# Loading a weight matrix with a cast in flight by GpSimd's software DMA instead of staging it and casting on engines

## The chip, the cores and the metric

The kernel runs on one core of a Trainium2 chip. The metric is device time in microseconds (us), the median of several executions. One execution of each kernel is also recorded by the hardware profiler; its span, from the first instruction to the last, is about 2 us shorter than the timed execution. In the profile PE is TensorE's matmuls, PEld its weight loads, DVE is VectorE, ACT ScalarE, POOL GpSimd, SP SyncE, and a "q" behind a name (SPq, POOLq) marks a queue of DMA issues. L1268 is line 1268 of the kernel. Lines of the changed kernel stand 4 further down than the same lines before, up to the place of the main edit (L911 before is L915 after); from there on the numbers agree again.

## The reference

Eight batches of linear attention (no softmax, RMS norm per head) followed by a residual MLP mixer with affine scalings. Cut to what matters:

```python
def _attn_ref(q, k, v, g_norm):                     # (8, 8, 576, 64)
    kv = np.einsum('bhsd,bhse->bhde', k, v)
    out = np.einsum('bhsd,bhde->bhse', q, kv)
    rms = np.sqrt(np.mean(out * out, axis=-1, keepdims=True) + 1e-06)
    return out / rms * g_norm

def _moe_ref(x, alpha1, beta1, w_tok, alpha2, beta2, w_ch1, w_ch2, lam):
    a1 = alpha1 * x + beta1                         # x: (8, 576, 512)
    tok = np.einsum('ts,bsd->btd', w_tok, a1)       # token mixing
    u = x + lam * tok
    a2 = alpha2 * u + beta2
    ch = np.maximum(a2 @ w_ch1, 0.0) @ w_ch2        # w_ch1 (512, 2048), w_ch2 (2048, 512)
    return u + lam * ch
```

All inputs are fp32. The two channel products run in bf16 on TensorE, so W_ch1 must be cast, and W_ch2 is multiplied by lam and cast at once.

## The kernel before

The program is not written in issue order. Operations are recorded with costs, priorities and dependencies, and a scheduler in the kernel's own Python simulates the engines with these costs and fixes a **static order** for each engine. Every engine then works through its list strictly in order and waits on semaphores where a dependency is on another engine or a DMA. An operation that may run on several engines is given to whichever seems best.

The scheduler's model of DMA is a single line of work that serves loads one after the other in the order of issue:

```python
if pick.lat is not None:                 # a DMA
    if e == "SP":
        dma_free = max(dma_free, t + (2.5 if t < 3 else 1.25)) + pick.lat
        pick.end = dma_free + 1.3        # when it believes the data is there
    ...
```

Both weights of the channel MLP pass through one staging tile of three 1 MB blocks. Four column slices of W_ch1 come first, then four row blocks of W_ch2:

```python
stg = sb("stg", [128, 3, 4, 512], F32)
w1  = sb("w1",  [128, 4, FF], BF16)
w2  = sb("w2",  [128, 16, DM], BF16)
...
order = ["k0", "v0", "q0", "k1", "t0", "v1", "q1", "t1",       # SyncE's first loads
         "w0", "g", "w1", "w2", "Bk", "Bv", "t2", "w3", "Bq", "lam", "a2", "w4",
         "w5", "w6", "w7"]
...
def load_w(i):
    if i < 4:                                                   # W_ch1
        P.op("SP", 0.6, lambda e: e.dma_start(stg[:, i % 3], moe_w_ch1[...]),
             w=[("stg", i % 3)], dma_us=2.6, at=sp["w%d" % i])
        for dj in range(4):                                     # 16 casts in all
            P.op({"ACT": ..., "POOL": 0.66, "DVE": ...}, 0, lambda e, dj=dj: copy(
                e, w1[:, dj, 512 * i:512 * i + 512], stg[:, i % 3, dj]), ...)
    else:                                                       # W_ch2
        n = i - 4
        P.op("SP", 0.6, lambda e: e.dma_start(stg[:, i % 3], moe_w_ch2[...]),
             w=[("stg", i % 3)], dma_us=2.6, at=sp["w%d" % i])
        for hh in range(4):                                     # 16 multiplies, VectorE or GpSimd
            P.op(dve_pool(512), 0, lambda e, hh=hh: e.tensor_tensor(
                out=w2[:, 4 * n + hh, :], in0=stg[:, i % 3, hh], in1=lam_bc[:], op=ALU.mult),
                r=[("stg", i % 3), "lam"], w=[("w2p", n, hh)], pri=60, after=u0, port=True)
```

VectorE's list holds the operations that TensorE waits for: it evacuates `ps`, the tiles that TensorE's matmuls write, for the first channel product (`ht`, L911), for K^T V (`kvr`, L494), for Q^T (`qtr`, L494) and for the small token weights (`wt`, L494). Where nothing useful is ready early on, the scheduler puts filler matmuls (L1334, 45 in the trace, 0.27 us each) on TensorE so that it does not idle.

Of the kernel before, what the change touches and what calls it, by code (L numbers as in the profile page):

```python
# [54 lines left out]
class Prog:  # L55
# [79 lines left out]
    def schedule(self):  # L135
# [83 lines left out]
        while left:  # L219
            progressed = False  # L220
            for e, q in queues.items():
                while q and free[e] <= t + 1e-9:
# [64 lines left out]
                    if pick.lat is not None:  # L287
                        if e == "SP":
                            dma_free = max(dma_free, t + (2.5 if t < 3 else 1.25)) + pick.lat
                            pick.end = dma_free + 1.3  # L290
                        else:
                            pick.end = t + pick.lat + 3.0
                    else:
                        pick.end = free[e] + (0.35 if e == "PE" else 0.15)
# [22 lines left out]
    def synchronize(self):  # L317

        known = {}
        pos = {}  # L320
        pool = None
        for o in self.sequence:
            e = self.queue_of(o.eng)
            if e == "POOL":

                if pool is not None:
                    o.deps.add(pool)
                pool = o
            o.pos = pos.get(e, 0)
            pos[e] = o.pos + 1  # L330
            k = known.setdefault(e, {})
            need = {}
            for y in o.deps:
                ye = self.queue_of(y.eng)
                if y.lat is not None:
                    key, v = ("dma", y.idx), 1
                else:
                    key, v = ye, y.pos + 1
                    if ye == e and e == "PE":
                        continue  # L340
                if v > need.get(key, (0, None))[0]:
                    need[key] = (v, y)
            for key, (v, y) in sorted(need.items(), key=lambda kv: -kv[1][1].end):
                if k.get(key, 0) >= v:
                    continue
                o.waits.append(y)
                y.inc = True
                for kk, vv in y.clock.items():
                    if vv > k.get(kk, 0):
                        k[kk] = vv  # L350
            o.clock = dict(k)
            if o.lat is not None:
                o.clock[("dma", o.idx)] = 1
                o.inc = True
            else:
                o.clock[e] = o.pos + 1

    def emit(self):
        nc = self.nc
        sems = {e: self.stack.enter_context(nc.semaphore("s_" + e)) for e in self.COMPUTE}  # L360
        count = {e: 0 for e in self.COMPUTE}
        val = {}
        dma = []
        for o in self.sequence:
            if o.lat is not None:

                for s in dma:
                    if o.clock.get(("dma", s[2]), 0):
                        break
                else:  # L370
                    s = [self.stack.enter_context(nc.semaphore("d%d" % len(dma))), 0, 0]
                    dma.append(s)
                s[1], s[2] = s[1] + 16, o.idx
                val[o.idx] = (s[0], s[1])
            elif o.inc:
                count[o.eng] += 1
                val[o.idx] = (sems[o.eng], count[o.eng])
        block = self.stack.enter_context(nc.Block("main"))

        @block.gpsimd  # L380
        def _(gps):
            for o in self.sequence:
                eng = self.eng[o.eng]
                for y in o.waits:
                    eng.wait_ge(*val[y.idx])
                ins = o.fn(eng)
                if o.lat is not None:
                    ins.then_inc(val[o.idx][0], 16)
                elif o.inc:
                    ins.then_inc(sems[o.eng], 1)  # L390
            for s in dma:
                nc.sync.wait_ge(s[0], s[1])
# [11 lines left out]
def bass_transnormer_attn__then__resmlp_affine_kernel(  # L404
# [15 lines left out]
    with ExitStack() as stack:  # L420
# [55 lines left out]
        def dve_us(n, mode=1):  # L476
            return 0.16 + n / 960.0 / mode

        def act_us(n):
            return 0.19 + n / 1200.0  # L480
# [554 lines left out]
        def params():  # L1035
# [34 lines left out]
            for x, (p, c) in enumerate(((64, 4), (0, 9))):  # L1070
                for i in range(2):
                    P.op("SP", 0.6, lambda e, i=i, p=p, c=c: e.dma_start(
                        rt[p + i:p + i + 1, c, :].rearrange("o (j p) -> o j p", p=128),
                        ebf[:, i, :]), r=["ebh", "ebl", "rtz"], w=[("rtc", x, i)], dma_us=0.05,
                        at=sp["w0"] + 0.1 + 0.01 * (2 * x + i))
                P.lastw[("rtc", x)] = [y for i in range(2) for y in P.lastw[("rtc", x, i)]]

        def params_late():
            for key in ("e1r", "lamr", "gr", "er", "ebh", "ebl", ("pc", 0), ("pc", 1)):
                for n in range(4):  # L1080
# [2 lines left out]
                            P.readers.get(key, []) + P.lastw[key])  # L1083

        order = ["k0", "v0", "q0", "k1", "t0", "v1", "q1", "t1",
                 "w0", "g", "w1", "w2", "Bk", "Bv", "t2", "w3", "Bq", "lam", "a2", "w4",
                 "w5", "w6", "w7"]
        sp = {n: i - 1000.0 for i, n in enumerate(order)}

        load_params()  # L1090
# [150 lines left out]
        for key in [("wst", tc) for tc in range(4)]:  # L1241
            for o in P.readers.get(key, ()):
                for j in range(16):
                    P.readers.setdefault(("ht", j), []).append(o)
                    for i in range(2):
                        P.readers.setdefault(("hth", j, i), []).append(o)

        def load_w(i):
            if i < 4:
                P.op("SP", 0.6, lambda e: e.dma_start(  # L1250
                    stg[:, i % 3], moe_w_ch1[:, 512 * i:512 * i + 512].rearrange(
                        "(j p) f -> p j f", p=128)), w=[("stg", i % 3)], dma_us=2.6,
                    at=sp["w%d" % i])
                for dj in range(4):
                    P.op({"ACT": act_us(512), "POOL": 0.66, "DVE": dve_us(512, 1.6)}, 0,
                         lambda e, dj=dj: copy(
                        e, w1[:, dj, 512 * i:512 * i + 512], stg[:, i % 3, dj]),
                        r=[("stg", i % 3)], w=[("w1p", i, dj)], at=-960.0 + i, port=True)
                P.lastw[("w1", i)] = [y for dj in range(4) for y in P.lastw[("w1p", i, dj)]]
                bias_groups(i)  # L1260
            else:
                n = i - 4
                P.op("SP", 0.6, lambda e: e.dma_start(
                    stg[:, i % 3], moe_w_ch2[512 * n:512 * n + 512, :].rearrange(
                        "(j p) c -> p j c", p=128)), w=[("stg", i % 3)], dma_us=2.6,
                    at=sp["w%d" % i])
                for hh in range(4):
                    P.op(dve_pool(512), 0, lambda e, hh=hh: e.tensor_tensor(  # L1268
                        out=w2[:, 4 * n + hh, :], in0=stg[:, i % 3, hh], in1=lam_bc[:],
                        op=ALU.mult), r=[("stg", i % 3), "lam"], w=[("w2p", n, hh)], pri=60,  # L1270
                        after=u0, port=True)
                P.lastw[("w2", n)] = [y for hh in range(4) for y in P.lastw[("w2p", n, hh)]]
# [98 lines left out]
```

## Time and profile before

| before | value |
|---|---|
| time, median of 3 first runs (range) | 363.12 us (363.04 to 363.73) |
| span of the profiled run, mean granted TensorE clock | 362.2 us, 0.995 |
| TensorE idle between 15.5 and 58.3 us (start-up with W_ch1) | 0.56 us |
| first weight load of the second channel layer | 58.10 us |
| end of the last matmul of that layer | 358.56 us |
| between these two | 300.47 us |

The layer's first 512-column matmul starts 0.21 us after its weight load. The lines of the page and of the stretches are shown and read in the prediction below. One view that the prediction did not use belongs here, because the outcome turns on it: the order of VectorE around the W_ch2 multiplies. Columns are start, length from the first start to the last end, engine, line, operation, output and inputs, count, and in brackets the idle time just before with what ended it.

```profile
37.58 4.20 DVE L911 TENSOR_SCALAR ht<-ps,bias 128x256 bf16<-128x256 f32 x6 [0.48 <-PE ps L952]
...
43.23 0.69 DVE L1268 TENSOR_TENSOR w<-stg,xtl 128x512 bf16<-128x512 f32 x1 [0.26 <-DMA stg<-in_moe_w_ch_dram]
...
43.91 1.89 DVE L1268 TENSOR_TENSOR w<-stg,xtl 128x512 bf16<-128x512 f32 x3
45.83 0.88 DVE L494 CAST kvr<-ps 64x256 fp32r<-64x256 f32 x2
```

The first multiply comes behind six evacuations of the first channel layer in a row, and three more just ahead of those, and its block lands 0.26 us after VectorE is free for it. The match is close, and VectorE loses almost nothing. In the staging view that the prediction quotes in part, the whole wait of VectorE for W_ch2 blocks is 0.3 us.

### The profile page before, as it was taken

The numbers are of one execution on the slowest core, as the hardware profiler recorded it, in microseconds if no ns is written. First come the engines' busy times: TensorE is split into PE (matmuls) and PEld (weight loads), VectorE is DVE, ScalarE is ACT, GpSimd is POOL, SyncE is SP. The second block draws the span as 40 slices with busy tenths as digits, with TensorE's granted clock in tenths as the row PEclk, the third lists the DMA queues.
The fourth block names the chain that finished last, engine by engine and source line by source line (L and its number), as shares of the span: only waits on it lengthen the run. The fifth ranks groups of instructions, "written<-read, shape, count | busy, mean of one in ns | idle before, by whom it ended". The sixth has DMA issues, their size and how long they took to land.

```text
span 362.2 us, 7967 instructions
## 1 busy us (share of the span) xinstructions
PE 353.6 (98%) x3543; PEld 213.6 (59%) x3335; DVE 207.1 (57%) x321; ACT 147.5 (41%) x262; POOL 113.1 (31%) x93
## 2 busy tenths in 40 slices
PE   7999999999999999999999999999999999999995
PEld 5888774467754554457744554457744554457644
DVE  3555799962876288723974289714883288620021
ACT  2576267037750168007830167007720156007500
POOL 4377078410252006700381016800751006300000
PEclk9899999999999999999999999999999999999999
DMA  7999996067947694667926692686746510341023
GB/s 282 364 375 338 376 365 223 0 73 128 315 156 119 107 313 162 88 128 117 381 47 134 111 352 88 116 119 194 288 66 128 115 29 2 72 93 24 2 58 87
DMA packets 67558, 59.17 MB, mean 163 GB/s; under 512 B 45552, under 2 KB 45828, under 8 KB 67524
## 3 DMA queue, kind: packets, MB, share of 16 engines
q1 hardware_dynamic: 67472, 58.66, 59.7%
q8 instruction: 27, 0.44, 0.5%
q14 instruction: 7, 0.06, 0.0%
q10 hardware_dynamic: 52, 0.01, 0.0%
HBM read 38.60 MB, written 9.44 MB: 133 GB/s over the span
## 4 chain that ended last, share of the span: by engine, by line
PE 93%; DMA 3%; DVE 1%; SPq 1%; issue 1%
PE ps L986 34%; PE ps L936 19%; PE ps L921 14%; PE ps L785 8%; PE ps L602 5%; DMA vf<-in_v_dram 3%; PE ps L397 2%; PE ps L682 2%; PE ps L1144 2%; PE ps L798 1%; PE ps L819 1%; PE ps L570 1%; PE ps L952 1%; DVE w L1268 1%; SPq L506 1%
## 5 line engine op out<-in xcount | busy, mean ns | idle before, releaser
L986 PE MATMUL ps<-w,ht 128*128 128x512 bf16 (+1 forms) x569 | 125.8, 373 | 1.8 <-issue 1.0
L986 PEld LDWEIGHTS ps<-w,ht 128*128 128x128 bf16 x592 | 56.8, 98 | 64.0 <-issue 1.2
L910 ACT ACTIVATE ht<-ps,bias 128x640 bf16<-128x640 f32 (+2 forms) x100 | 74.1, 744 | 45.8 <-PE ps L936 37.9
L936 PE MATMUL ps<-a2t,w 128*128 128x320 bf16 x512 | 71.5, 299 | 0.0
L760 POOL TENSOR_TENSOR xm<-xm,g_bc 128x1024 f32<-128x1024 f32 (+1 forms) x17 | 35.0, 2061 | 111.4 <-DVE rt L757 109.3
L936 PEld LDWEIGHTS ps<-a2t,w 128*128 128x128 bf16 x512 | 49.4, 98 | 20.2
L997 DVE TENSOR_TENSOR xm<-ps,xm 128x512 f32<-128x512 f32 (+1 forms) x33 | 22.2, 673 | 56.5 <-PE ps L986 56.4
L921 PE MATMUL ps<-a2t,w 128*128 128x512 bf16 x231 | 53.3, 380 | 0.9 <-DVE small L737 0.5
L633 ACT ACTIVATE kvd<-ps 64x256 bf16<-64x256 f32 x24 | 9.1, 378 | 101.2 <-PE ps L602 101.0
L731 DVE TENSOR_REDUCE small<-sq 128x16 f32<-128x1024 f32 (+3 forms) x30 | 25.1, 849 | 24.9 <-ACT sq L729 24.7
L921 PEld LDWEIGHTS ps<-a2t,w 128*128 128x128 bf16 x240 | 22.6, 98 | 25.7 <-DVE xm L753 0.7
L785 PE MATMUL ps<-rt,wt 128*128 128x512 bf16 x140 | 31.4, 379 | 0.0
L911 DVE TENSOR_SCALAR ht<-ps,bias 128x512 bf16<-128x512 f32 (+2 forms) x32 | 22.9, 725 | 11.4 <-PE ps L921 5.1
L729 ACT ACTIVATE sq<-ps 128x1024 f32<-128x1024 f32 (+3 forms) x30 | 21.6, 735 | 10.2 <-PE ps L397 8.2
L769 DVE TENSOR_TENSOR xm<-ps,xm 128x512 f32<-128x512 f32 x28 | 19.1, 686 | 8.0 <-PE ps L785 7.9
L785 PEld LDWEIGHTS ps<-rt,wt 128*128 128x128 bf16 x140 | 13.7, 98 | 16.5
L771 POOL TENSOR_TENSOR a2b<-xm,a_bc 128x512 bf16<-128x512 f32 x11 | 17.7, 1610 | 17.6 <-DVE xm L769 17.6
L534 POOL TENSOR_TENSOR qs<-qf,qs 128x512 bf16<-128x512 f32 x12 | 15.2, 1266 | 25.5 <-ACT qs L493 24.5
L997 DVE TENSOR_TENSOR xtl<-ps,xtl 128x512 f32<-128x512 f32 x4 | 2.8, 691 | 35.5 <-PE ps L986 35.5
L753 DVE TENSOR_TENSOR xm<-ps,small 128x1024 f32<-128x1024 f32 (+1 forms) x20 | 20.0, 1004 | 0.2
L602 PEld LDWEIGHTS ps<-vf,kf 64*64 64x64 f32 x1152 | 18.0, 137 | 3.5 <-issue 2.5
L602 PE MATMUL ps<-vf,kf 64*64 64x64 f32 x1152 | 19.3, 223 | 0.3 <-DMA vf<-in_v_dram 0.2
(105 smaller groups left out, 337.1 us busy)
## 6 DMA issues: line engine op xcount, KB each, us to landing
stg<-in_moe_w_ch_dram SPq DMA_DIRECT2D x8, 1024.0 KB, 10.9
kf<-in_k_dram SPq DMA_DIRECT2D x7, 1152.0 KB, 6.2
vf<-in_v_dram SPq DMA_DIRECT2D x7, 1152.0 KB, 9.2
qf<-in_q_dram SPq DMA_DIRECT2D x7, 1152.0 KB, 9.8
out_dram<-xm SPq DMA_DIRECT2D x62, 128.0 KB, 2.4
kf<-in_k_dram SPq DMA_DIRECT2D x2, 576.0 KB, 5.8
vf<-in_v_dram SPq DMA_DIRECT2D x2, 576.0 KB, 7.1
qf<-in_q_dram SPq DMA_DIRECT2D x2, 576.0 KB, 8.5
```

Source lines behind the costliest of these rows:

```text
L602: m = e.matmul(t.ap(slice(64 * i, 64 * i + 64))[:, y, 64 * x_:64 * x_ + 64], kf[rows, x, c], vf[rows, x, c], start=(c == 0), stop=(c == 8) ...
L729: P.op("ACT", act_us(64 * m), lambda e: e.activation(both(sqv), raw(), ACT.Square), r=[t], w=[("sq", sqs)])
L731: P.op("DVE", dve_us(64 * m), lambda e: e.tensor_reduce(out=smv, in_=sqv, axis=AX.X, op=ALU.add), r=[("sq", sqs)], w=[("sm", sms)], pri=-20)
L753: P.op("DVE", dve_us(64 * m), lambda e: e.tensor_tensor(out=x3, in0=raw(), in1=inv(), op=ALU.mult), r=[t, ("sm", sms)], w=xk, pri=-200)
L760: P.op(dve_pool(64 * m) if b < 2 else "POOL", pool_us(64 * m), lambda e: e.tensor_tensor(out=x3, in0=x3, in1=gb, op=ALU.mult), r=xk + ["g" ...
L785: m = e.matmul(t.flat(), wt[:, sc if sc < 4 else 4 + b % 2, 128 * c:128 * c + 128], rt[:, rs(b, sc), :], start=(sc == 0), stop=(sc == 4))
L910: return e.activation(dst, src(), ACT.Relu, bias=bi)
L911: return e.tensor_scalar(out=dst, in0=src(), scalar1=bi, scalar2=0.0, op0=ALU.add, op1=ALU.max)
L921: m = e.matmul(t.flat(), w1[:, dj, 128 * fj:128 * fj + 128], a2t[:, dj, 0:512], start=(dj == 0), stop=(dj == 3))
L936: m = e.matmul(t.ap()[:, i, 0:320], w1[:, dj, 128 * fj:128 * fj + 128], a2t[:, dj, 320 * i:320 * i + 320], start=(dj == 0), stop=(dj == 3))
L986: m = e.matmul(t.flat()[:, 0:m_], ht[:, fj, 128 * c:128 * c + 128], w2[:, fj, lo:hi], start=(fj == 0), stop=(fj == 15))
L997: P.op("DVE", dve_us(m_), lambda e: e.tensor_tensor(out=x, in0=t.flat()[:, 0:m_], in1=x, op=ALU.add), r=[t] + keys, w=keys)
```

## The change

The intent is to give up the staging and the 16 engine casts for W_ch1. GpSimd issues four DMAs that read fp32 and write bf16 straight into the weight tile. The staging tile is then free for W_ch2 from the start, and the scheduler may move everything else into the room. Its core:

```diff
                         if e == "SP":
                             dma_free = max(dma_free, t + (2.5 if t < 3 else 1.25)) + pick.lat
                             pick.end = dma_free + 1.3
+                        elif e == "POOL":
+                            dma_free = max(dma_free, free[e] + 1.0) + pick.lat
+                            pick.end = dma_free + 1.3
...
         order = ["k0", "v0", "q0", "k1", "t0", "v1", "q1", "t1",
-                 "w0", "g", "w1", "w2", "Bk", "Bv", "t2", "w3", "Bq", "lam", "a2", "w4",
-                 "w5", "w6", "w7"]
+                 "g", "t2", "Bk", "Bv", "lam", "a2", "w4",
+                 "Bq", "w5", "w6", "w7"]
...
+        gate = [("vf", 1), ("wst", 3), ("w1", 0), ("w1", 1)]
+
         def load_w(i):
             if i < 4:
-                P.op("SP", 0.6, lambda e: e.dma_start(
-                    stg[:, i % 3], moe_w_ch1[...]), w=[("stg", i % 3)], dma_us=2.6, at=sp["w%d" % i])
-                for dj in range(4):
-                    P.op({"ACT": ..., "POOL": 0.66, "DVE": ...}, 0, lambda e, dj=dj: copy(
-                        e, w1[:, dj, 512 * i:512 * i + 512], stg[:, i % 3, dj]), ...)
-                P.lastw[("w1", i)] = [...]
+                P.op("POOL", 1.2, lambda e: e.dma_start(
+                    w1[:, :, 512 * i:512 * i + 512], moe_w_ch1[
+                        :, 512 * i:512 * i + 512].rearrange("(j p) f -> p j f", p=128)),
+                    w=[("w1", i)], dma_us=2.6, at=-9000.0 + i, after=P.lastw[gate[i]])
                 bias_groups(i)
```

The rest of the diff (cut here) gives each GpSimd DMA a semaphore of its own, keeps these DMAs out of GpSimd's chain of self-waits, and moves one small parameter copy on SyncE.

More of the change, by code (lines that the diff above doesn't have):

```diff
@@ L327, in synchronize @@
                     o.deps.add(pool)
-                pool = o
+                if o.lat is None:
+                    pool = o
             o.pos = pos.get(e, 0)
@@ L367, in emit @@
                 for s in dma:
-                    if o.clock.get(("dma", s[2]), 0):
+                    if o.eng != "POOL" and not s[3] and o.clock.get(("dma", s[2]), 0):
                         break
                 else:
-                    s = [self.stack.enter_context(nc.semaphore("d%d" % len(dma))), 0, 0]
+                    s = [self.stack.enter_context(nc.semaphore("d%d" % len(dma))), 0, 0, o.eng == "POOL"]
                     dma.append(s)
@@ L1074, in params @@
                         ebf[:, i, :]), r=["ebh", "ebl", "rtz"], w=[("rtc", x, i)], dma_us=0.05,
-                        at=sp["w0"] + 0.1 + 0.01 * (2 * x + i))
+                        at=sp["t1"] + 0.5 + 0.01 * (2 * x + i))
                 P.lastw[("rtc", x)] = [y for i in range(2) for y in P.lastw[("rtc", x, i)]]
@@ L1246, in bass_transnormer_attn__then__resmlp_affine_kernel @@
                         P.readers.setdefault(("hth", j, i), []).append(o)
+        gate = [("vf", 1), ("wst", 3), ("w1", 0), ("w1", 1)]
         def load_w(i):
             if i < 4:
-                P.op("SP", 0.6, lambda e: e.dma_start(
-                    stg[:, i % 3], moe_w_ch1[:, 512 * i:512 * i + 512].rearrange(
-                        "(j p) f -> p j f", p=128)), w=[("stg", i % 3)], dma_us=2.6,
-                    at=sp["w%d" % i])
-                for dj in range(4):
-                    P.op({"ACT": act_us(512), "POOL": 0.66, "DVE": dve_us(512, 1.6)}, 0,
-                         lambda e, dj=dj: copy(
-                        e, w1[:, dj, 512 * i:512 * i + 512], stg[:, i % 3, dj]),
-                        r=[("stg", i % 3)], w=[("w1p", i, dj)], at=-960.0 + i, port=True)
-                P.lastw[("w1", i)] = [y for dj in range(4) for y in P.lastw[("w1p", i, dj)]]
+                P.op("POOL", 1.2, lambda e: e.dma_start(
+                    w1[:, :, 512 * i:512 * i + 512], moe_w_ch1[
+                        :, 512 * i:512 * i + 512].rearrange("(j p) f -> p j f", p=128)),
+                    w=[("w1", i)], dma_us=2.6, at=-9000.0 + i, after=P.lastw[gate[i]])
                 bias_groups(i)
```

## The prediction

Three things in it are estimates, which the trace of the kernel before does not show: the 1.2 us of one issue on GpSimd (the cost that the change writes into the scheduler), the landing of slice 0 at 22.5 us, and the half of 361 GB/s that a casting load gets beside SyncE's queue.

> **What bounds the kernel now.** I read the engine shares first, then the chain that ended last, then TensorE's waits, then stretches of time, and last the staging buffer that the change empties.
>
> The page of the kernel before, its engine line and its chain:
>
> ```profile
> PE 353.6 (98%) x3543; PEld 213.6 (59%) x3335; DVE 207.1 (57%) x321; ACT 147.5 (41%) x262; POOL 113.1 (31%) x93
> ...
> PE 93%; DMA 3%; DVE 1%; SPq 1%; issue 1%
> ```
>
> The chain says the same as the busy share: 93% of the path is matmuls, and the one large DMA piece in it is the load of V's second half at the start. Busy time of matmuls can hide slack, so I checked lengths: 16 matmuls of 512 columns after the start-up took 3.40 us, 0.21 us each, in the middle and at the end alike. TensorE is really working.
>
> All of TensorE's waits over the whole span:
>
> ```profile
> PE ps L1334 <- DVE eps L1113: 1.1, 1, 1.1
> PE ps L986 <- issue: 1.0, 6, 0.2
> PE ps L921 <- DVE small L737: 0.5, 1, 0.5
> PE ps L1053 <- DMA w<-in_moe_beta_dram: 0.4, 1, 0.4
> PE ps L570 <- DMA qf<-in_q_dram: 0.4, 1, 0.4
> PE ps L602 <- DMA vf<-in_v_dram: 0.2, 1, 0.2
> ```
>
> No wait names a cast of W_ch1 or its loads. The stretches of the span (columns: length, then busy us and count of PE, PEld, DVE, ACT, POOL, then TensorE clock, DMA share, GB/s):
>
> ```profile
> 0.00:15.50 15.50, 13.29 (x216) 10.90 (x217) 6.19 (x17) 5.82 (x14) 4.61 (x17) 0.96 0.90 329
> 15.50:58.30 42.80, 42.24 (x518) 33.75 (x520) 30.85 (x69) 25.63 (x60) 27.05 (x27) 0.98 1.01 361
> 80.00:358.60 278.60, 276.51 (x2590) 157.79 (x2366) 150.12 (x203) 109.59 (x177) 71.40 (x43) 1.00 0.56 134
> ```
>
> From 15.5 to 58.3 us, where W_ch1 is loaded, cast and first used, TensorE is busy 42.24 of 42.80 us, while the DMA engines are also full (share 1.01, 361 GB/s). Two things are saturated, but only TensorE is on the path.
>
> The staging buffer's instructions (duration min/median/max, first and last start):
>
> ```profile
> L493 ACT ACTIVATE w<-stg x9: 614/620/630, 22.2 to 36.3; 128x512 bf16<-128x512 f32 x9
> L494 POOL CAST w<-stg x7: 609/614/614, 23.3 to 36.5; 128x512 bf16<-128x512 f32 x7
> ```
>
> These 16 casts are what the change removes. None ran on VectorE.
>
> [...] The before-trace has no GpSimd-issued load and can't show its cost. [...]
>
> **The change, part by part.**
>
> Removed: 9 ACT casts x 0.620 + 7 POOL casts x 0.614 = 9.9 us of engine time between 22 and 37 us. On the path: nothing, since no TensorE wait goes back to them.
>
> Bytes: the source is still 4 x 1 MB of fp32 in HBM. Only the write side halves. The DMA-bound phase is reordered, not shortened.
>
> TensorE: the same matmuls. What is to be gained from 15.5 to 58.3 us is its idle time, 0.56 us, plus the filler matmuls that the scheduler sets where it expects a gap: 3 at 28.7 us and 1 at 32.9 us, about 0.12 us each (3 took 0.35), 0.5 us in all. **The ceiling is about 1.1 us, 0.3%.** The built order of the changed kernel is identical on TensorE until 25 us; after that it has 7 fillers for 4, so the scheduler itself expects slightly more gap: +0.35 us. Against that, the 0.5 us wait on VectorE at 55 us should go, because the W_ch2 multiplies start before 40 us (staging is free sooner) instead of piling up at 43 to 54 us: -0.4 us. Sum about zero.
>
> Added: four issues in GpSimd's queue, each ahead of arithmetic that TensorE needs. Call one issue D. I choose D = 1.2 us as an estimate ([...]what the kernel's own scheduler assumes). The GpSimd chain, with durations from the before-trace (1.27 us for a 128x512 product, 0.72 for the 64-row one, 0.07 between):
> - Issue 1 waits for V's second half, landed about 13.5 us: done 14.7. First token product 14.8 to 16.0 (before: 14.77 to 16.04; nothing lost).
> - Issue 2 waits for the fourth piece of w_tok. By bytes, 4.72 MB (six K/V/Q halves of 0.59, w_tok 1.18) at 329 GB/s is 14.3 us; with the slice taking a share and the landing I put 17.5. Done 18.7; two products and one scaling: 22.1.
> - Issue 3 waits for slice 0. At half of 361 GB/s 1.05 MB takes 5.8 us[...]. Done 23.7; a scaling to 25.0; the second half's token products done at 26.3, 27.6 and 28.4.
> - TensorE wants these at about 30.3, 30.7 and 32.0: in the before-trace it is at 25.1 us where both orders still agree; 20 token matmuls and 10 sums (3.6 us), bias matmuls 0.4, 8 transposes 0.9 and three fillers follow.
>
> Slack about 3 us. Two issues lie in that chain whichever way it is followed, so D may reach about 2.7 us before TensorE stalls; beyond it each further us costs about two.
>
> Data: slice 0 is wanted at about 28.7 us (lands 22.5), slice 1 at 33 (about 27), slices 2 and 3 at about 45 and 47 (30 to 40). Batch 1's Q now stands behind four W_ch1 slices, its own K and V, the parameters and a W_ch2 block: 14.2 MB in all; 5.1 MB have moved by 15.5 us, the other 9.1 MB take 25.2 us: 40.7 us, wanted at 44.4. Everything fits, Q with the least room.
>
> After 58 us nothing is touched but the static order; TensorE idles 2.1 of 278.6 us there, which may come out a few tenths different.
>
> Sum: 363.1 + 0.35 - 0.4, plus 0.3 that I add for the lopsided risk on GpSimd: **363.3 us**.
>
> **The rivals.**
> 1. *GpSimd becomes the bound of the start-up.* The issue is dearer than 1.2 us (each slice has 4 rows of 1 KB per partition, 512 runs)[...]. For it: GpSimd was already busy 8.9 of 10 us between 20 and 30 us and works in order. Against: 4.3 us of casts leave it. With D = 4: 2 x 1.3 = 2.6 us, 366 us; for 2% D must exceed 6 us.
> 2. *The casting transfer is slow, or takes bandwidth from the main queue.* Issue 3 waits on slice 0, so a landing beyond about 25.6 us (11 us of transfer) stalls TensorE one for one. Or w_tok and Q land later. For it: the engines are full. Against: 3 to 4 us of room everywhere. At worst 365 to 368 us.
> 3. *The freed ACT and POOL time pays off.* Feeding is earlier, fillers and gaps vanish: 362 us. Against: the 1.1 us ceiling, and more fillers in the order, not fewer.
>
> **Range and chances.** The floor is the ceiling on gain plus noise in the later order: 361.7. The upper side is D near 4 us or a slow slice: 367.0. Faster by over 2% would need 7.3 us where 1.1 is to be had: 0.01. Slower by over 2% needs D above 6 us or a slice taking some 18 us: 0.05. Within 2%: 0.94.
>
> **What would show it.** Right: TensorE's waits again hold no entry above 1 us between 15 and 58 us; its busy time moves by under 1 us; ACT loses 9 casts and POOL 7; the DMA share stays near 1.0 to about 55 us. The first matmul of the early channel groups starts near 34 us, and the 512-column second-layer matmuls near 58 us, as before. The GpSimd queue shows four issues, near 13.5, 17.5, 22.5 and 31 us. Wrong: a wait of TensorE, or of VectorE ahead of it, on the token products or scalings of GpSimd near 29 to 32 us (rival 1); on the bias matmuls or on batch 1's Q (rival 2); or a lower granted clock after such a gap, which would add to it. The clock already dips to 0.55 between 14 and 16 us in the before-trace, in an order of TensorE that the change leaves alone; if that dip moves, 1 us may go either way.

## The result, and the profile after

| | before | after |
|---|---|---|
| time, median of 4 runs (range) | 363.43 us (363.04 to 364.51) | 376.02 us (373.06 to 378.01) |
| ratio of fast runs, 95% interval | | 1.0335 (1.0246 to 1.0424) |
| profiled run: span, granted clock | 362.2 us, 0.995 | 372.3 us, 0.991 |
| TensorE idle, 15.5 to 58.3 us | 0.56 us | 4.63 us |
| first second-layer weight load | 58.10 us | 65.08 us |
| end of the last second-layer matmul | 358.56 us | 368.82 us |
| between these two | 300.47 us | 303.74 us |

The change made the kernel 3.4% slower. A ratio, here and below, is the mean time of one kernel's fast runs over that of the other's of the same rounds, so it is not quite the ratio of the medians in the table. Executions over 1.5% slower than the fastest of the same kernel are left out of the means.

The engine line and the chain of the changed kernel's page:

```profile
PE 359.3 (97%) x3578; PEld 213.5 (57%) x3338; DVE 207.9 (56%) x318; ACT 141.2 (38%) x253; POOL 120.5 (32%) x93
...
PE 77%; DMA 15%; DVE 4%; SPq 3%; issue 0%; DVEq 0%
```

TensorE's share is still 97%, and by that line alone nothing has happened. The chain tells otherwise: 15% of the path now runs through DMAs and 7% through VectorE and SyncE's queue; before, these were 3%, 1% and 1%. ACT fell by its 9 casts. GpSimd's count is unchanged: 7 casts less, 4 DMA issues more, and 3 operations that moved over from VectorE.

TensorE's waits (releaser: total, times, longest):

```profile
PE ps L940 <- DVE xm L757: 1.9, 2, 1.5
PE ps L574 <- DVE qtr L498: 1.4, 1, 1.4
PE ps L606 <- issue: 1.3, 1, 1.3
PE ps L925 <- DVE ht L915: 1.3, 1, 1.3
PE ps L1334 <- DVE eps L1117: 1.1, 1, 1.1
PE ps L606 <- DMA vf<-in_v_dram: 0.7, 1, 0.7
PE ps L1191 <- DVE wt L498: 0.6, 1, 0.6
```

Apart from the 1.1 us at the very start, which before has too, and the wait for V, these are new. Four of them name VectorE. None names GpSimd's token products, Q by more than 0.2 us, or a W_ch1 slice, which were the places that the prediction watched.

The start-up by stretches (columns as in the prediction):

```profile
15.50:58.30 42.80, 38.17 (x486) 30.26 (x486) 28.02 (x54) 18.52 (x44) 23.43 (x20) 0.92 1.02 303
```
```profile
50.00:52.00 2.00, 1.38 (x8) 0.94 (x6) 1.95 (x3) 0.38 (x1) 1.86 (x2) 0.50 1.04 406
```

TensorE is busy 4 us less, and its clock, the third number from the end, is 0.50 in the later part: the trace's own clock records put half clock from 48.95 to 55.78 us. The fall from 361 to 303 GB/s is not a slower transfer, as the share of the engines (1.02) shows: the bytes counted for the casting loads are those written, 2.10 MB on the page's software queue for 4.19 MB of fp32, while the page's HBM read is 38.60 MB in both kernels.

### The start-up: VectorE stands at its own next instruction

Who ended VectorE's idle time? Its order in the changed kernel, same columns as before:

```profile
36.36 2.36 DVE L1268 TENSOR_TENSOR w<-stg,xtl 128x512 bf16<-128x512 f32 x2 [2.15 <-DMA stg<-in_moe_w_ch_dram]
38.65 0.86 DVE L915 TENSOR_SCALAR ht<-ps,bias 128x256 bf16<-128x256 f32 x2
...
44.57 2.96 DVE L1268 TENSOR_TENSOR w<-stg,xtl 128x512 bf16<-128x512 f32 x3 [3.40 <-DMA stg<-in_moe_w_ch_dram]
47.45 0.41 DVE L498 CAST wt<-ps 128x256 bf16<-128x256 f32 x1
47.79 3.35 DVE L1268 TENSOR_TENSOR w<-stg,xtl 128x512 bf16<-128x512 f32 x2
51.16 0.88 DVE L498 CAST kvr<-ps 64x256 fp32r<-64x256 f32 x2
52.05 0.69 DVE L498 CAST qtr<-ps 128x512 fp32r<-128x512 f32 x1
```

The multiplies by W_ch2 have moved forward in the static list, ahead of the evacuations of the first channel layer (L915). VectorE arrives at the first at 34.2 us and stands 2.15 us until the block lands; it arrives at the second block's multiplies at 41.2 us and stands 3.40 us. The two multiplies after 47.79 us take 1.7 us each where one alone takes 0.68; GpSimd is multiplying at the same time. All that while evacuations that are ready wait behind: `ht` until 38.65, `wt` until 47.45, `kvr` until 51.16, `qtr` until 52.05 us. These are three of the releasers in TensorE's list. The staging tile's view sums who waited for it (total us, times):

```profile
  POOL w L1268: 11.4, 3
  DVE w L1268: 5.6, 2
```

The blocks do not land later than before. The first lands at 36.4 us where before it was 43.2. What moved further is their place in the list. Run without the chip, the kernel's own scheduler believes that the four blocks land at 33.2, 38.8, 41.4 and 49.2 us; the first three land at 36.4, 44.6 and about 47.6, so 3.2, 5.8 and 6.2 us after its belief. For before it believes 41.4 and 44.0 for the first two and the trace shows 43.2 and about 46.0, some 2 us late each. The extra lateness fits an error of the single-line model (e4 below tests it): it puts W_ch1 slices 2 and 3 last (44.0 and 46.6 us), as they are issued late. On the chip they are served beside SyncE's queue, not behind it; their last packets end at 34.4 and 42.2 us, though needed only at about 49 and 55. From 22 to 32 us the trace counts 194 GB/s on SyncE's queue and 94 GB/s written (188 read) on GpSimd's.

### Later: stores behind loads on SyncE

The other 3.3 us (303.74 against 300.47) are lost after the start-up, in code that the change does not touch. SyncE's timeline halfway through the program, first of the changed kernel (start, length, queue, line, operation, output and input, count):

```profile
170.44 1.23 SPq L1006 DMA_DIRECT2D out_dram<-xm  x2
171.71 0.59 SPq L510 DMA_DIRECT2D kf<-in_k_dram  x1
172.35 0.54 SPq L510 DMA_DIRECT2D vf<-in_v_dram  x1
172.93 0.51 SPq L510 DMA_DIRECT2D qf<-in_q_dram  x1
173.49 1.47 SPq L1006 DMA_DIRECT2D out_dram<-xm  x2
```

then of the kernel before:

```profile
167.41 2.51 SPq L1002 DMA_DIRECT2D out_dram<-xm  x4
169.96 0.60 SPq L506 DMA_DIRECT2D kf<-in_k_dram  x1
170.61 0.56 SPq L506 DMA_DIRECT2D vf<-in_v_dram  x1
171.21 1.31 SPq L506 DMA_DIRECT2D qf<-in_q_dram  x1
```

Before, all four stores of 128 KB go ahead of the next batch's 3.5 MB of loads. After, two of them go behind, and land 11.7 and 11.2 us after their issue, where the median of all such stores on the page is 2.4 us. The buffer that they empty is written next by a product on VectorE, whose line in the changed kernel's timeline is:

```profile
185.61 1.23 DVE L757 TENSOR_TENSOR xm<-ps,small 128x1024 f32<-128x1024 f32 x1 [2.90 <-DMA out_dram<-xm]
```

TensorE waits 1.5 us for it there and 0.3 us in a later batch (the first entry of its waits). The start-up's new pattern has shifted the scheduler's arrangement for the whole program.

### The profile page after: what moved, and what is told of

Its sections match the earlier page's. It is cut to its first block, busy times and chain, and to the rows that moved or that the text cites.

```text
span 372.3 us, 7999 instructions
## 1 busy us (share of the span) xinstructions
PE 359.3 (97%) x3578; PEld 213.5 (57%) x3338; DVE 207.9 (56%) x318; ACT 141.2 (38%) x253; POOL 120.5 (32%) x93
## 2 busy tenths in 40 slices
DMA packets 67558, 57.07 MB, mean 153 GB/s; under 512 B 45552, under 2 KB 47876, under 8 KB 67524
## 3 DMA queue, kind: packets, MB, share of 16 engines
HBM read 38.60 MB, written 9.44 MB: 129 GB/s over the span
## 4 chain that ended last, share of the span: by engine, by line
PE 77%; DMA 15%; DVE 4%; SPq 3%; issue 0%; DVEq 0%
PE ps L990 34%; PE ps L925 13%; PE ps L940 11%; PE ps L789 8%; DMA out_dram<-xm 6%; DMA stg<-in_moe_w_ch_dram 6%; PE ps L606 4%; DMA qf<-in_q_dram 3%; DVE w L1268 2%; SPq L510 2%; PE ps L401 1%; PE ps L802 1%; PE ps L686 1%; PE ps L1148 1%; PE ps L696 1%; DVE xm L757 1%
## 5 line engine op out<-in xcount | busy, mean ns | idle before, releaser
L990 PE MATMUL ps<-w,ht 128*128 128x512 bf16 (+1 forms) x592 | 128.9, 373 | 0.0
L914 ACT ACTIVATE ht<-ps,bias 128x640 bf16<-128x640 f32 (+2 forms) x100 | 72.7, 732 | 48.6 <-PE ps L940 35.4
L940 PE MATMUL ps<-a2t,w 128*128 128x320 bf16 x512 | 72.4, 299 | 2.2 <-DVE xm L757 1.9
L764 POOL TENSOR_TENSOR xm<-xm,g_bc 128x1024 f32<-128x1024 f32 (+1 forms) x18 | 37.1, 2062 | 63.8 <-DVE rt L761 63.1
L925 PE MATMUL ps<-a2t,w 128*128 128x512 bf16 x240 | 55.8, 384 | 1.3 <-DVE ht L915 1.3
L925 PEld LDWEIGHTS ps<-a2t,w 128*128 128x128 bf16 x240 | 22.7, 99 | 27.2 <-DVE ht L915 2.2
L735 DVE TENSOR_REDUCE small<-sq 128x16 f32<-128x1024 f32 (+3 forms) x30 | 25.3, 853 | 14.0 <-ACT sq L733 13.7
L761 POOL TENSOR_TENSOR rt<-xm,e_bc 128x512 bf16<-128x512 f32 (+1 forms) x10 | 16.0, 1600 | 49.9 <-DVE xm L757 49.6
L915 DVE TENSOR_SCALAR ht<-ps,bias 128x512 bf16<-128x512 f32 (+2 forms) x32 | 24.3, 767 | 12.9 <-PE ps L940 6.4
L538 POOL TENSOR_TENSOR qs<-qf,qs 128x512 bf16<-128x512 f32 x10 | 13.6, 1356 | 49.9 <-ACT qs L497 49.4
L775 POOL TENSOR_TENSOR a2b<-xm,a_bc 128x512 bf16<-128x512 f32 x13 | 20.3, 1563 | 14.1 <-DVE xm L773 13.9
L757 DVE TENSOR_TENSOR xm<-ps,small 128x1024 f32<-128x1024 f32 (+1 forms) x20 | 19.9, 1005 | 5.9 <-DMA out_dram<-xm 5.7
L789 PEld LDWEIGHTS ps<-rt,wt 128*128 128x128 bf16 x140 | 13.7, 98 | 16.4
```

What stands on the lines that cost most here:

```text
L735: P.op("DVE", dve_us(64 * m), lambda e: e.tensor_reduce(out=smv, in_=sqv, axis=AX.X, op=ALU.add), r=[("sq", sqs)], w=[("sm", sms)], pri=-20)
L757: P.op("DVE", dve_us(64 * m), lambda e: e.tensor_tensor(out=x3, in0=raw(), in1=inv(), op=ALU.mult), r=[t, ("sm", sms)], w=xk, pri=-200)
L764: P.op(dve_pool(64 * m) if b < 2 else "POOL", pool_us(64 * m), lambda e: e.tensor_tensor(out=x3, in0=x3, in1=gb, op=ALU.mult), r=xk + ["g" ...
L789: m = e.matmul(t.flat(), wt[:, sc if sc < 4 else 4 + b % 2, 128 * c:128 * c + 128], rt[:, rs(b, sc), :], start=(sc == 0), stop=(sc == 4))
L914: return e.activation(dst, src(), ACT.Relu, bias=bi)
L915: return e.tensor_scalar(out=dst, in0=src(), scalar1=bi, scalar2=0.0, op0=ALU.add, op1=ALU.max)
```

## The experiments

Each ran beside the kernel before on the same chip; before's median there was 363.3 to 363.5 us. "Order kept" means that the edit is applied after the scheduler has fixed all orders.

| run | median us (range) | ratio (95%) | TensorE idle 15.5 to 58.3 | first second-layer weight load at | from there to the last |
|---|---|---|---|---|---|
| e1_no_w2_wait | 367.31 (367.01 to 368.41) | 1.0116 (1.0093 to 1.0140) | 1.32 | 58.87 | 302.84 |
| e2_before_order | 362.61 (361.82 to 363.79) | 0.9980 (0.9955 to 1.0004) | 0.00 | 56.33 | 300.47 |
| e3_told_landings | 366.03 (365.33 to 366.42) | 1.0069 (1.0050 to 1.0087) | 1.08 | 59.28 | 301.09 |
| e5_stores_first | 370.99 (368.41 to 375.67) | 1.0184 (1.0144 to 1.0224) | 6.36 | 65.27 | 300.47 |
| e9_before_order_again | 362.31 (362.11 to 363.72) | 0.9976 (0.9956 to 0.9997) | 0.00 | 56.14 | 300.47 |
| e6_before_again (one look) | 363.35 | | 0.00 | 57.58 | 300.47 |
| e7_after_again (one look) | 379.56 | | 5.66 | 69.84 | 304.37 |
| e8_gap | 373.80 (369.70 to 374.15) | 1.0259 (1.0204 to 1.0314) | 5.73 | 63.73 | 300.47 |
| e12_both | 365.63 (364.51 to 366.33) | 1.0074 (1.0045 to 1.0103) | 1.55 | 58.75 | 300.47 |
| e4_half_bytes | 369.72 (368.25 to 371.04) | 1.0176 (1.0138 to 1.0214) | 1.81 | 59.27 | 306.45 |
| e11_fewer_fillers | 374.82 (371.43 to 377.52) | 1.0249 (1.0213 to 1.0286) | 3.47 | 65.73 | 306.24 |

The first column is from all runs of a kernel, the ratio from fast ones alone; e5_stores_first had one slow run in four, e11_fewer_fillers two, and the trace of the latter is a slow one.

### e1_no_w2_wait: the changed kernel without the wait for W_ch2

Theory: VectorE's stand at the W_ch2 blocks costs the start-up. Rival: GpSimd's work on the issues or the casting transfers do. The multiplies read a resident tile of the same shape instead of the staging tile; loads, instructions and order stay. The result is wrong (relative error 0.217).

```diff
-                        out=w2[:, 4 * n + hh, :], in0=stg[:, i % 3, hh], in1=lam_bc[:],
+                        out=w2[:, 4 * n + hh, :], in0=e1_bc[:], in1=lam_bc[:],
...
         P.schedule()
+        for o in unwaited:                       # the 16 multiplies
+            o.deps.difference_update(w2_loads)
+            o.deps.update(P.lastw["e1"])
```

> Wrong result on purpose: the changed kernel with every engine's order kept, but the 16 multiplies that make W_ch2 read a tile that is resident since 14 us instead of the staging buffer; the W_ch2 loads still run. Theory A (the in-order VectorE queue stands on late W_ch2 blocks while the evacuations behind it are ready): TensorE's idle time from 15.5 to 58.3 us falls from 4.6 us to under 1.2 us, the second half-clock stretch at 49 to 56 us goes, the first second-layer matmul comes at 58 to 60 us instead of 65.3, and the time is 365 to 367 us (the 3 us lost after 165 us stay). Rival B (the casting loads slow the engines or the transfers that TensorE itself needs): time stays above 371 us with idle time above 3 us, its waits on other names. Rival C (the new static order by itself costs): 370 us or more with little idle time.

The first second-layer weight load starts at 58.87 us, 6.2 us earlier than in the changed kernel and 0.8 us later than before. The median and the idle time (1.32 us) came out just above the ranges expected. The half-clock stretch is gone from the trace, though one of the other three runs had a mean clock of 0.993. Of TensorE's waits those of L925 on `ht`, and those on `wt` and `qtr`, have gone; the two largest left after the start are:

```profile
PE ps L940 <- DVE xm L757: 1.6, 2, 1.3
PE ps L606 <- issue: 1.3, 1, 1.3
```

So the wait for W_ch2 carries 6.2 of the 7.0 us of the start-up loss, and in this trace the casting loads, all four still there, do not. The later loss stays (302.84), as it must if it belongs to SyncE's order.

### e2_before_order and e9_before_order_again: the casting loads alone

The kernel before with its own order on all engines; only then the 16 casts and four staging loads are taken out, and four casting loads are put into GpSimd's list. If the casting loads cost something by themselves, it shows here.

```diff
         P.schedule()
+        for i, start in enumerate((13.1, 16.8, 21.0, 30.6)):
+            o = Op("POOL", 1.2, lambda e, i=i: e.dma_start(w1[:, :, 512*i:512*i+512], moe_w_ch1[...]), ...)
+            o.deps = set(gate[i] if i < 2 else [new[i - 2]])
+            ...
+        P.ops = [o for o in P.ops if o not in gone]      # the casts and their loads
+        P.sequence = sorted(P.ops, key=lambda o: (o.start, o.idx))
```

> The change alone without its new order: the order of the kernel before on every engine, the 16 casts and 4 staging loads taken out, the four casting loads set into GpSimd's queue at the places they have in the changed kernel. Theory A: the multiplies of W_ch2 stand late in VectorE's queue as before and wait for nothing, so 362 to 364 us, TensorE idle under 1 us from 15.5 to 58.3 us. Rival B (the casting loads themselves cost: shared transfers, GpSimd's time): 367 us or more. Rival C: as theory A.

> The kernel of the second experiment again, with more rounds, because its interval (0.9955 to 1.0004) doesn't settle whether the casting loads gain anything. If the gain of 0.2% is real: 0.996 to 0.999 with an interval wholly under 1, TensorE without a gap from 15 us on. If it was chance: 0.999 to 1.001. Its trace also shows whether the half-clock stretch of the kernel before at 14 to 18 us is absent again.

TensorE's waits of the first of the two, complete, and its start-up:

```profile
PE ps L1339 <- DVE eps L1114: 1.1, 1, 1.1
PE ps L603 <- DMA vf<-in_v_dram: 0.4, 1, 0.4
```
```profile
15.50:58.30 42.80, 42.80 (x527) 33.42 (x526) 32.08 (x71) 22.22 (x52) 27.47 (x25) 1.00 1.08 328
```

TensorE does not idle at all in the start-up. GpSimd still waits 12.3 us for a W_ch2 block, and it harms nobody, while VectorE, whose multiplies stand late in its list, waits 0.5 us. With five rounds the version is 0.24% faster than before, an interval that just excludes 1. Comparing only runs whose mean clock was 0.998 or more, in which no half-clock stretch of 3.413 us, the shortest that ends inside a trace, can lie (it would make the mean 0.995), four of before average 363.0 us and eight of these two 362.3: 0.7 us. That is near the 0.56 us of idle time in before's first trace, but before's second trace (e6 below) has no idle time there at all, so where the 0.7 us come from is not shown. This version beats the kernel before by no more than that.

### e3_told_landings: tell the scheduler when the blocks land

The changed kernel, where the scheduler is told that the W_ch2 blocks land 3.5, 6.0, 6.5 and 3.0 us after its model's time, and then orders freely.

```diff
-                            pick.end = dma_free + 1.3
+                            pick.end = dma_free + 1.3 + pick.late
...
+                ld.late = (3.5, 6.0, 6.5, 3.0)[n]
```

> The changed kernel, only the scheduler's guess of when the four W_ch2 blocks land is moved to the landings measured (3.5, 6.0, 6.5 and 3.0 us later than it assumed), so it orders the engines anew. Theory A: the multiplies move back in VectorE's queue, start-up idle under 1.5 us, 362 to 367 us (the later part of the order is drawn anew and may lose or gain up to 3 us). Rivals B and C: above 370 us.

VectorE no longer appears among those who wait for the staging tile, the half clock is gone, and 10 of the 12.6 us are recovered: 366.03 us. Putting the landing times right in the model is therefore enough to recover most of the loss. It isn't a clean test of one part, since everything may move, and the later part, 301.09, came out different again.

### e5_stores_first: the later loss alone

The changed kernel, order kept, except that on SyncE after 150 us a K, V or Q load goes behind stores that stood up to 3.5 us behind it (three places).

```diff
+        for i, o in enumerate(sp_seq):
+            if o in big_loads and o.start > 150.0:
+                near = [y for y in sp_seq[i:] if y.start < o.start + 3.5 and y in stores]
+                if near:
+                    o.start = near[-1].start + 0.01 + 1e-4 * o.idx
```

> The changed kernel, order kept, only in SyncE's queue after 150 us the K, V and Q loads of the next batch go behind the two to four output stores that the changed order had put after them. If those stores, landing 11 us late behind 3.5 MB of loads, cause the loss after 165 us (two waits of TensorE on VectorE's normalising product, 1.5 and 0.3 us, and neighbours): 2 to 3 us less than the changed kernel in the same state of the clock, batches 4 to 6 each within 0.3 us of their length before (43.7, 38.0, 43.7 us). If not: no difference beyond 1 us.

From there to the last second-layer matmul it takes 300.47 us, as before to a hundredth (3.3 us less than in the changed kernel, where 2 to 3 were expected), and the wait on L757 has left TensorE's list. So SyncE's order is the whole of the later loss. The start-up keeps its loss; its idle time is 6.36 us here, of which 0.98 us is a wait that the changed kernel's trace doesn't have (see "What held" below).

### e12_both: the two removals together

e1's edit and e5's in one kernel (wrong result again), to see whether the two losses are all.

> Wrong result on purpose: the changed kernel's order with both suspected causes out at once, the W_ch2 multiplies not waiting for their blocks (first experiment) and the output stores ahead of the next loads (fourth). If the two causes are separate and are all of it but the 1.3 us gap in the K-transpose-V matmuls: 363.5 to 365 us, TensorE idle about 1.3 us from 15.5 to 58.3 us and none after, clock 1.0. If they overlap: above 366 us. If a third cost remains: above 365 us with idle time under another name.

The profiled run ends its matmuls 0.7 us after before's; the median is 2.3 us above. It came out a little above the range expected. What is left at the start in its trace is one stop of 1.3 us whose releaser is "issue"; the last experiment looks at it.

### e8_gap: what a gap of known size costs

The e2 version, with six fills of a scratch tile put into VectorE's list ahead of batch 1's `kvr` copies. It makes one stand of VectorE with nothing else changed, and asks how much more than the gap is lost.

```diff
+        for i in range(6):
+            o = Op("DVE", 0.9, lambda e: e.memset(scratch[:], 0.0), ...)
+            o.start = first - 0.002 + 0.0001 * i          # first: the first kvr copy
```

> The kernel of the second experiment (order of before, casting loads) with six fills of an unused tile, some 5.5 us in all, set into VectorE's queue ahead of batch 1's K-transpose-V copies at 45 us: a gap of TensorE made on purpose, no transfer and no byte changed. Theory A: a queue that stands for 5.5 us stops TensorE for about 3 to 4.5 us, and a half-clock stretch follows that adds 1 to 3 us: 366.5 to 370 us. If a gap doesn't bring the half clock: 365.5 to 367 us with clock 1.0. If VectorE's queue has that much slack: under 364 us, and theory A loses its ground.

```profile
53.29 1.86 PE L927 MATMUL ps<-a2t,w 128*128 128x512 bf16 x4 [5.73 <-DVE kvr L496]
```
```profile
50.00:52.00 2.00, 0.00 (x0) 0.00 (x0) 1.57 (x2) 0.00 (x0) 1.92 (x2) 0.50 1.05 406
```

TensorE idles 5.7 us, the clock halves from 49.8 to 56.7 us, and the median is 11.2 us above the e2 version's first median, about twice the gap. The expectation was too low. The profiled run was the mildest of the four (clock 0.990, 369.70 us); the other three had clocks of 0.975 to 0.982 and 373.6 to 374.2 us. A single stand of VectorE in the start-up thus suffices for a loss of the size of the changed kernel's, and most of its spread is granted clock.

### e6_before_again and e7_after_again: the clock in another execution

Both kernels unchanged, one look each, for the clock records.

> The kernel before once more, for a second trace. If its half-clock stretch at 14 to 18 us belongs to the kernel, it is there again (mean clock 0.995, span 362 to 363 us); if it is chance, it may be gone, and the span is then 1 to 2 us shorter.

> The changed kernel once more, for a second trace. TensorE's gaps between 37 and 53 us (waits on VectorE behind the W_ch2 multiplies, 4 to 5 us in all) are there again. The half-clock stretch after them should explain the spread from 373 to 378 us: about half its length is lost, so a span of 371 goes with some 3.4 us at half clock and one of 376 with some 13 us.

Before had its half clock from 14.3 to 17.7 us again. The changed kernel had the same waits as in its first trace, with the one on `qtr` at 2.4 us instead of 1.4, and half clock for 13.7 us, 54.0 to 67.7, instead of 6.8. The 13.7 us ran on although TensorE never paused in them.

### e4_half_bytes: fewer bytes ahead of W_ch2

The changed kernel, order kept, each casting load bringing only 256 of its 512 columns; GpSimd fills the rest with zeros at about 9 to 14 us. The content is wrong, though inside tolerance. If W_ch2 is late because it shares the engines with the slices, half the slice bytes must bring it forward.

```diff
-                    w1[:, :, 512 * i:512 * i + 512], moe_w_ch1[:, 512 * i:512 * i + 512]...
+                    w1[:, :, 512 * i:512 * i + 256], moe_w_ch1[:, 512 * i:512 * i + 256]...
```

> Wrong result on purpose: the changed kernel, order kept, each casting load brings only half of its columns (0.5 MB read for 1 MB), the rest filled once by GpSimd while it is idle at 9 to 14 us. Theory A in its bandwidth part: the W_ch2 blocks are late because 4 MB of W_ch1 go out before and among them; with 2 MB less at about 360 GB/s they land some 3 to 6 us earlier (the second at 39 to 41 us instead of 44.6), VectorE waits for them under 2 us, and the time is 367 to 371 us. If bytes have nothing to do with it (the casting loads are slow by themselves, or issue is the limit): landings within 1 us of the changed kernel's and 373 us or more.

Hit. The second stand of VectorE is:

```profile
40.08 2.98 DVE L1268 TENSOR_TENSOR w<-stg,xtl 128x512 bf16<-128x512 f32 x3 [0.92 <-DMA stg<-in_moe_w_ch_dram]
```

The second block lands at 40.1 us instead of 44.6, VectorE waits 0.9 us in all instead of 5.6, and the start-up ends at 59.27. So the bytes of the slices are part of what makes W_ch2 late. The later loss is larger here (306.45), because the store wait grew to 2.6 us and half clock followed at 183.2 us.

### e11_fewer_fillers: the "issue" gap

In the changed kernel, e1, e5, e7 and e12, TensorE stops for 1.3 to 1.45 us within the 144 small matmuls of K^T V at about 45 us, with "issue" as the releaser: no wait that the profile shows. In e1 a 16 KB fetch on the instruction queue begins at 42.65 us and TensorE resumes at 44.98, in the changed kernel 44.25 and 46.67. (In e3 and e4 it stops there for 0.5 and 0.8 us.) The theory is that TensorE has run out of instructions. e1 with 27 of its first 30 fillers removed, which takes 54 instructions (with their weight loads) out of the stream ahead, should move the gap to another matmul.

```diff
+        cut = set(fill[3:30])
+        P.ops = [o for o in P.ops if o not in cut]
```

> Wrong result on purpose: the first experiment's kernel with 27 of the 30 filler matmuls at 1 to 6 us taken out, so that every later TensorE instruction stands 54 instructions earlier in its stream. The 1.3 us gap inside the 144 K-transpose-V matmuls at 45 us came at the same matmul in three traces, each time 2.3 to 2.4 us after a 16 KB instruction fetch began. If the gap is TensorE waiting for its next instructions: it leaves its place (gone, or at another instruction), and the time may fall by up to 1.3 us from 367.3; a colder start before 13 us costs nothing, as V ends the wait there. If it is anything in the data: the gap stays at the same matmul.

```profile
49.56 0.56 PE L1191 MATMUL ps<-wt,smask 128*128 128x64 bf16 x5 [3.20 <-issue]
```

The gap did leave the K^T V group and came at the next line, 2.5 us after a fetch that began at 47.0 us. It follows the place in the stream. The fetches of 16 KB are in the traces (27 packets, 0.44 MB on the instruction queue of the changed kernel's page). That the fetch is what ends the gap is argued from the timing, not shown. But the timing is close: in all eight traces that have the gap (after, e1, e3, e4, e5, e7, e11, e12) TensorE resumes 2.3 to 2.5 us after the fetch begins, while the gap itself is anything from 0.5 to 3.2 us long. The other expectation, that a start with fewer fillers ("colder") costs nothing, was wrong: TensorE waited 4.1 us for V, and the early channel groups began at 35.9 instead of 33.6 us. Its time can't be used for more.

## Why the prediction was wrong

The prediction said 363.3 us and at most 367.0, and within 2% with a chance of 0.94. The measured 376.02 is outside.

**What held.** The ceiling on the gain: 1.1 us predicted, about 1.06 us found between medians in e9, and 0.7 us between runs at full clock (whether it comes from the idle time that the ceiling counted is not shown). GpSimd's chain: one issue took 0.80 to 0.93 us where 1.2 was chosen, as its row shows,

```profile
L1256 POOL DMA_DIRECT2D w<-in_moe_w_ch_dram x4: 803/804/927, 13.9 to 31.9; - x4
```

the four issues came at 13.9, 17.6, 22.2 and 31.9 us (13.5, 17.5, 22.5 and 31 predicted), the token products were in time, and the early channel groups began at 33.6 us (34 predicted). The data that TensorE reads itself was there. Rivals 1 and 2 did not happen in the changed kernel's two traces, and with the casting loads and the old order TensorE does not idle. One other trace does show them: in e5's, slice 0 landed at 23.2 us instead of the changed kernel's 21.1 (22.5 predicted), GpSimd's third issue waited for it, VectorE's sum waited for GpSimd's scaling, and TensorE for the sum:

```profile
23.73 0.80 POOL L1259 DMA_DIRECT2D w<-in_moe_w_ch_dram  x1 [1.84 <-DMA w<-in_moe_w_ch_dram]
32.35 1.09 DVE L838 TENSOR_TENSOR xm<-ps,xm 128x256 f32<-128x256 f32 x3 [0.92 <-POOL xm L767]
32.83 0.66 PE L859 MATMUL ps<-ident,xm 128*128 128x128 f32 x4 [0.98 <-DVE xm L838]
```

The slack there was not the 3 us of the prediction, which ended GpSimd's chain at the token products and left out the scalings behind them (which its own signs of rival 1 do name): in the changed kernel's trace that scaling ended at 30.5 us and the sum that reads it began at 32.1, 1.6 us later.

**The step that failed first** is "Everything fits" at the end of the data step. It checked every load against the time at which *TensorE* wants it, and left out W_ch2, which TensorE needs late but VectorE meets early. In the step on TensorE's matmuls I had even read from the built order that "the W_ch2 multiplies start before 40 us", and booked it as a gain of 0.4 us. An in-order engine that reaches an instruction earlier than its data is blocked there. The landing of the blocks was never worked out against their new place in VectorE's list; on the chip it is 36.4 us against an arrival at 34.2, and 44.6 against 41.2. The 0.4 us of gain was 5.6 us of standing for VectorE, and +7.0 us at the first second-layer matmul.

**The second step** is "After 58 us nothing is touched but the static order", put at "a few tenths". The static order was the thing touched. Two stores behind 3.5 MB of loads cost 3.3 us (near 171 us; loads ahead of stores stand in two later places too), and e5 shows that this is all of it.

**The caveat on the clock** named the right kind ("a lower granted clock after such a gap, which would add to it") but carried no size. In the traces the clock is 0.50 or 1.00, and the half-clock stretches last 3.413 us (before), 6.827 (after) and 13.653 (e7), which is 1, 2 and 4 times 3.413. One unit of 3.413 us at half clock costs at most 1.7 us (half of it), and the mean clock of 0.9953 over 362 us of before's trace is one such unit. By that reading, an estimate from the mean clocks, after's four runs (0.994, 0.991, 0.982, 0.982) hold about 1, 2, 4 and 4 units, which orders their spans of 371.3, 372.3, 376.1 and 376.2 us. The dip at 14 to 16 us that the prediction warned of is in both traces of before and in neither of the changed kernel.

**The rivals' list** had a GpSimd, a DMA and a gain case, but not "the freed staging tile lets other work be ordered too early", though it is the most direct effect of emptying a buffer.

**The sum.** A rough account at full clock uses runs whose mean clock is 0.998 or more (means over 5 runs of before on the chip of e12 and 4 on the other; 3 of e1; one each of e5 and e12, so it is good to some tenths only):

| part | how | us |
|---|---|---|
| W_ch2 waits | e5 over its before (368.4 - 363.0), less e12 over its own (364.5 - 362.7) | 3.6 |
| stores behind loads | e1 over its before (367.2 - 363.0), less the same 1.8 | 2.4 |
| left with both removed | e12 over its before; 1.3 of it is the "issue" gap in the trace | 1.8 |
| half clock in the median run | after's median over before at full clock (376.0 - 363.0), less the three above | 5.2 |

The last line is what remains, not a measurement, but it is 3 units of 1.7 us, in the midst of the 1 to 4 units that the clocks show.

## What to carry to other kernels

When a change frees a buffer, ask which instructions a scheduler will now place earlier, and check the data's landing against the time at which each *in-order engine* arrives at them, not only against the time at which the bound engine needs the result. A static order made from a DMA model is only as good as that model: when a transfer moves to a second queue that is served side by side (here 194 and 188 GB/s read), re-measure the landings, or keep the old order and change only the transfer, as the version that did best here. And on a kernel with TensorE at 98% busy, price a gap at up to twice its length, as e8's 5.7 us cost 11.2: the clock may halve after it.

## What the traces show of the clock, the queues and the fetches

- When the clock fell to half, the pause of TensorE before it had lasted 2.9 us at most (in e11), and the changed kernel's longest before its fall was 1.3 us. I cut six traces (after, e7, e5, e8, e4, e11) into windows of 3.413 us (the length of before's half-clock stretch) aligned with their clock changes and added TensorE's idle time in each, as far as modelled matmul ends allow. Seven windows at full clock with 1.71, 1.98, 2.01, 2.11, 2.29, 2.41 and 2.89 us of idle were followed by half clock; windows with 1.47 us and less were not. Exceptions stand: one with 2.99 us of idle in the first 5 us of e11's trace was not followed by it, nor were those with 1.54 and 1.78 us at the ends of e11's and e4's, and the half clock at 14 to 15 us in both traces of before and in e11's follows windows with 0.6 us of idle or less. The cause of that early stretch is open.
- In e7 13.653 us ran at half clock with TensorE fully busy (four 512-column matmuls took 1.93 us there and 1.03 just before, in the changed kernel's first trace 1.91 at 53.70 us and 1.04 at 56.96, which agrees with the clock record), in before 3.413 us. Why they differ is open.
- GpSimd's own occupation by one issue of a 128-partition, 512-run slice was 0.80 to 0.93 us. From 22 to 32 us the DMA engines moved 194 GB/s on SyncE's queue beside 188 GB/s read (94 written) on GpSimd's.
- Gaps of 0.5 to 3.2 us on TensorE each ended 2.3 to 2.5 us after a 16 KB fetch began, seven of them on a stretch of 144 small matmuls and e11's at the line after it. That the fetch ends them is inference.
- A profile's GB/s counts the written bytes of a casting load: 57.07 MB on the page after against 59.17 before, for the same 38.60 MB read from HBM.
